# Retention followed by a multiplicative feed-forward layer: three w_out loads moved to ScalarE's queue, first weight products reordered

## Chip, core and metric

The kernel runs on one core of a Trainium2 chip. Its engines work side by side, each on its own list of instructions in program order: TensorE (PE in the profile: matmuls and transposes into PSUM; PEld is its weight load), VectorE (DVE), ScalarE (ACT), GpSimd (POOL) and SyncE (SP, which here only issues DMAs). The metric is the device time in microseconds (us). The time before is the median of three runs.

## What is computed

The first part is a recurrent retention over 4 batches, 8 heads, 768 tokens and head size 64, the second a feed-forward layer with a product of two projections, on 3072 tokens:

```python
gamma = 1.0 - 2.0 ** (-5.0 - np.arange(H))
for t in range(S):
    state = gamma * state + einsum('bhd,bhe->bhde', k[:, :, t], v[:, :, t])
    y[:, :, t] = scale * einsum('bhd,bhde->bhe', q[:, :, t], state)
x = y.transpose(0, 2, 1, 3).reshape(3072, 512)
a = x @ w1                # 512 x 1024
b = x @ w2                # 512 x 1024
h = (a * b) @ w3          # 1024 x 1024
out = h @ w_out           # 1024 x 512
```

All inputs and the output are float32; the matmuls take float16.

## The kernel before

**Tiling.** The tokens are cut into 12 chunks of 256, three to a batch. For each chunk the kernel computes retention as masked scores plus a carried state, then the products with w1 and w2, their elementwise product, and one last product. Since nothing stands between w3 and w_out, it multiplies these two once, at the start: W3O = w3 @ w_out, 1024 x 512, kept as eight tiles of 128 rows (`W3O[f]`).

**How W3O is made (lines 257 to 298).** Blocks of w3 and w_out come in as float32, 512 KB each, in staging tiles `st`: `r0` to `r7` are 128 rows of w3 (`load_rows`, line 107), `wo0` to `wo3` are 256 rows of w_out, two to a partition (`load_wo`, line 112). For each w3 block f there are these steps:

- `cast_w3(f, engs)` casts it to float16 (`w3h`, line 61 through `copy`; "vs" means the left half on VectorE and the right half on ScalarE).
- `turn_w3(f, bank)` turns it with eight transposes on TensorE (line 274).
- `turned_w3(f, eng)` copies the turned block from PSUM to SBUF (`w3t`, line 61).
- `w3_mm(f, i)` multiplies it with w_out block i, which `cast_wo(i, eng)` has cast (`wo`); two matmuls of 512 columns, line 290. Four of these, i = 0 to 3 in any order, sum up one `W3O[f]`, which `w3_out` copies out.

So `w3_mm(f, i)` needs both the turned block f and the cast block i. "S0", "X0", "K" and so on are names of PSUM banks.

**What sets the order.** The schedule is written out by hand (lines 696 to 1375): each engine executes its instructions in the order in which these calls emit them, and waits where its operand is not there yet. Lines 696 to 728 emit the loads: each of the `fetch` calls is one or more DMAs, all issued by SyncE, in this order: r4, wo0, r1, r2, wo1, r5, wo2, r3, r6, r7, k0, wo3, q0 (four DMAs), v0, r0, q1 (four), k1, v1, then the blocks of w1 and w2, then later tokens. There are 18 staging tiles. Lines 729 to 848 are the stage in which W3O is made, later mixed with the retention of chunks 0 and 1. `warm(m)` (line 674) issues m matmuls on zeros whose results nobody reads. `identity`, `numbers`, `arguments` and `tables` (lines 730 to 733) prepare constants; `tables` is the first thing on ScalarE: five activations of the function Exp (lines 233 and 235). `late_numbers` and `step_decays` are further constants on GpSimd.

Of the kernel before, what the change touches and what calls it, by code (L numbers as in the profile page):

```python
# [20 lines left out]
def kernel(  # L21
# [11 lines left out]
    nc = tc.nc  # L33
# [26 lines left out]
    def copy(eng, dst, src):  # L60
        {"v": nc.vector.tensor_copy, "g": nc.gpsimd.tensor_copy, "s": nc.scalar.copy}[eng](dst, src)  # L61

    def split(engs, dst, src):
        w = 1024 // len(engs)
        for j, eng in enumerate(engs):
            copy(eng, dst[:, j * w : (j + 1) * w], src[:, j * w : (j + 1) * w])
# [4 lines left out]
    def bank(tag, shape, dtype=FP):  # L71
        return psum.tile(shape, dtype, tag=tag, name="ps" + tag)
# [3 lines left out]
    def new_stage():  # L76
        return stage.tile([128, 1024], FP, tag="st", name="st")
# [4 lines left out]
    def load(nm, n, via=None):  # L82
        via = via or nc.sync
        b, c = divmod(n, PER)
        t = new_stage()
        src = source[nm][b, :, c * T : (c + 1) * T, :]
        if nm == "q" and n < EO:
            for a in range(NP):
                via.dma_start(
                    t[a : 128 : NP, :].rearrange("u (r x) -> u r x", r=2),  # L90
                    src[2 * a : 2 * a + 2, :, :].rearrange("r (u j) d -> u r (j d)", j=8),
                )
        elif nm == "q" or n < EO:
            via.dma_start(
                t[:, :].rearrange("p (h x) -> p h x", x=2 * D), src.rearrange("h (p t) d -> p h (t d)", t=2)
            )
        else:
            for s in range(2):
                via.dma_start(  # L99
                    t[:, s * 512 : (s + 1) * 512].rearrange("p (h d) -> p h d", d=D),  # L100
                    src[:, s * 128 : (s + 1) * 128, :].rearrange("h i d -> i h d"),
                )
        tok_in[nm, n] = t

    def load_rows(src, i):
        t = new_stage()
        nc.sync.dma_start(t[:, :], src[i * 128 : (i + 1) * 128, :])  # L107
        return t

    def load_wo(i):  # L110
        t = new_stage()
        nc.sync.dma_start(
            t[:, :].rearrange("p (t n) -> p t n", t=2),
            moe_w_out[i * 256 : (i + 1) * 256, :].rearrange("(p t) n -> p t n", t=2),
        )
        return t

    w3_st, wo_st, w_st = {}, {}, {}

    def fetch(names):  # L120
        for x in names.split():
            kind, i = x[:-1], int(x[-1])
            if kind == "r":
                w3_st[i] = load_rows(moe_w3, i)
            elif kind == "wo":
                wo_st[i] = load_wo(i)
            elif kind in ("w1", "w2"):
                w_st[kind, i] = load_rows({"w1": moe_w1, "w2": moe_w2}[kind], i)
            else:
                load(kind, i)  # L130
# [19 lines left out]
    def need(*x):  # L150
        assert done.issuperset(x)
# [26 lines left out]
    def late_numbers():  # L178
        done.add("late_numbers")

        nc.gpsimd.iota(tok_i[:, :, :], pattern=[[128, 2], [0, H]], base=1 - 128, channel_multiplier=1)
        for g in range(2):
            nc.gpsimd.iota(
                pos_i[:, g, :, :].rearrange("p s (t i) -> p s t i", t=2), pattern=[[128, 2], [1, 2], [2, 32]],
                base=1 - 128 + 64 * g, channel_multiplier=0,
            )
        nc.gpsimd.memset(keep64[:, :], 1.0)
        for g in range(2):
            rows = slice(g * 64, g * 64 + 64)
            nc.gpsimd.affine_select(  # L190
                out=keep64[rows, :], in_=keep64[rows, :], compare_op=GE, fill=0.0,
                base=0, pattern=[[1, 2], [2, 32]], channel_multiplier=-1,
            )
# [43 lines left out]
    def step_decays():  # L237
        done.add("decays")
        for h in range(H):
            r, p = (h % 2) * 64, h // 2  # L240
            nc.gpsimd.memset(GS[r : r + 64, p, :], gam[h] ** T)
# [18 lines left out]
    def cast_wo(i, eng):  # L260
        done.add(("wo", i))
        split(eng, WO[i][:, :, :].rearrange("p a n -> p (a n)"), wo_st[i][:, :])

    def cast_w3(f, eng):
        w3h[f] = att.tile([128, 1024], HP, tag="kq"[len(w3h_tags) % 2] + "16", name="w3h", bufs=3)
        w3h_tags.append(f)
        split(eng, w3h[f][:, :], w3_st[f][:, :])

    def turn_w3(f, tag):
        need("identity")  # L270
        src, ps = w3h.pop(f), bank(tag, [128, 1024], HP)
        for g in range(8):
            c0 = g // 2 * 256 + g % 2
            nc.tensor.transpose(ps[:, g * 128 : (g + 1) * 128], src[:, c0 : c0 + 255 : 2], ident16[:, :])  # L274
        w3p[f] = ps

    def turned_w3(f, eng):
        w3t[f] = fsb.tile([128, 1024], HP, tag="pa", name="w3t", bufs=8)
        copy(eng, w3t[f][:, :], w3p.pop(f)[:, :])

    def w3_mm(f, i, tag=None, first=False, last=False):
        need(("wo", i))
        if first:
            acc[f] = bank(tag, [128, DM])
            w3n[f] = 0
        w3n[f] += 2
        assert last == (w3n[f] == 8)
        for r in range(2):
            g = 2 * i + r
            nc.tensor.matmul(  # L290
                acc[f][:, :], lhsT=w3t[f][:, g * 128 : (g + 1) * 128], rhs=WO[i][:, r, :],
                start=(first and r == 0), stop=(last and r == 1),
            )
# [377 lines left out]
    def warm(m, tag="X1"):  # L671
        ps = bank(tag, [128, 512])
        for _ in range(m):
            nc.tensor.matmul(ps[:, :], lhsT=zeros[:, 0:128], rhs=zeros[:, :], start=True, stop=True)
# [15 lines left out]
    def evac(w, n, u, eng="s"):  # L690
        if w == "a":
            a_evac(n, u, ab.pop((w, n, u)), eng)
        else:
            b_evac(n, u, ab.pop((w, n, u)))

    fetch("r4")
    fetch("wo0")
    fetch("r1")
    fetch("r2")
    fetch("wo1")  # L700
    fetch("r5")
    fetch("wo2")
    fetch("r3")
    fetch("r6")
    fetch("r7")
# [32 lines left out]
    warm(3, "F2")  # L738
    turned_w3(4, "v")
    cast_wo(0, "s")  # L740
    warm(1, "F2")
    step_decays()
    cast_w3(1, "v")
    w3_mm(4, 0, "S0", first=True)
    cast_w3(2, "gs")
    turn_w3(1, "S1")
    warm(3, "F2")
    turned_w3(1, "v")
    turn_w3(2, "X0")
    warm(2, "F2")  # L750
    cast_wo(1, "g")
    w3_mm(1, 0, "S1", first=True)
    w3_mm(1, 1)
    warm(1, "F2")
    turned_w3(2, "v")
    w3_mm(2, 1, "X0", first=True)
    cast_wo(2, "g")
    cast_w3(5, "sv")
    late_numbers()
    w3_mm(4, 1)  # L760
    turn_w3(5, "X1")
    turned_w3(5, "v")
    w3_mm(1, 2)
    cast_w3(3, "s")
    w3_mm(2, 2)
    w3_mm(5, 2, "X1", first=True)
# [1 line left out]
    w3_mm(5, 0)  # L768
    turn_w3(3, "K")
    fetch("v3")  # L770
    w3_mm(4, 2)
    w3_mm(2, 0)
    turned_w3(3, "s")
    turn_w3(6, "F0")
    w3_mm(5, 1)
# [630 lines left out]
```

## Time and profile before

| | |
|---|---|
| median of 3 runs | 181.64 us (180.94 to 182.09) |
| the profiled execution's own time | 181.46 us |
| its span in the profile | 179.7 us |
| TensorE busy in the span | 172.8 us (96%) |
| VectorE, ScalarE, GpSimd busy | 100.1, 67.9, 64.5 us |
| moved by DMA | 40.22 MB, mean 224 GB/s |
| first DMA issue, SyncE | 0.81 us after the start |

The span is the time between the first and last instruction that the profile records; 1.76 us of the execution lie outside it. A line of the timeline gives the start, the duration, the engine, the line of the kernel, the operation, what it writes and reads, and in brackets how long the engine was idle before and what ended this idle time. The chain of waits starts from the last instruction and goes back, at each step to what released it.

### The profile page before, as it was taken

To read this page: it belongs to the slowest core of one execution; us is meant where nothing else is said; L and a number is where in the kernel's file an instruction comes from. 1 tells how busy PE (TensorE), PEld (TensorE's weight loads), DVE (VectorE), ACT (ScalarE), POOL (GpSimd) and SP (SyncE) were. 2 spreads that over 40 slices of the span, in tenths; PEclk is the share of its full clock that TensorE was granted. 3 is DMA by queue.
4 is the path that set the end of the run, shared out by engine and by line. 5 is a ranking of instruction groups with operands and counts; after the bars stand their busy time and mean duration, and the time that the engine had idled before them with its cause. 6 is when DMAs were issued, how large, how long until landed. Compare 5 with 4: busy or idle time off the path is not lost.

```text
span 179.7 us, 6033 instructions
## 1 busy us (share of the span) xinstructions
PE 172.8 (96%) x2626; PEld 123.7 (69%) x2626; DVE 100.1 (56%) x172; ACT 67.9 (38%) x120; POOL 64.5 (36%) x93
## 2 busy tenths in 40 slices
PE   7699999999999999999999999999999999999993
PEld 2245556578856785885877858768688587786872
DVE  2342779762966487548367384464654836634330
ACT  4425537790237332322314314232232231332422
POOL 7545056576242752724437045062450500000000
PEclk9999999999999999999999999999999999999999
DMA  5999999999999999999999999999999982250303
GB/s 201 364 420 364 357 312 364 406 348 233 177 259 239 213 173 221 202 196 237 150 209 266 196 237 231 210 280 209 237 255 264 108 277 67 81 156 4 117 0 117
DMA packets 80025, 40.22 MB, mean 224 GB/s; under 512 B 59392, under 2 KB 73984, under 8 KB 80000
## 3 DMA queue, kind: packets, MB, share of 16 engines
q1 hardware_dynamic: 80000, 39.85, 92.2%
q8 instruction: 20, 0.33, 0.8%
q14 instruction: 5, 0.04, 0.1%
HBM read 29.36 MB, written 6.29 MB: 198 GB/s over the span
## 4 chain that ended last, share of the span: by engine, by line
PE 75%; DMA 12%; SPq 4%; ACT 3%; POOL 2%; DVE 1%; issue 1%; POOLq 0%
PE psF L573 38%; PE psF L630 20%; DMA st<-in_moe_w_out_dram 5%; DMA st<-in_v_dram 4%; DMA st<-in_k_dram 3%; SPq L99 2%; PE psX L509 2%; PE psK L290 2%; PE psF L290 2%; PE psX L290 2%; PE psX L536 2%; PE psS L394 1%; ACT pa L61 1%; POOL v L69 1%; PE psS L290 1%; SPq L107 1%
## 5 line engine op out<-in xcount | busy, mean ns | idle before, releaser
L573 PE MATMUL psF<-xt,w 128*128 128x256 f16 x640 | 71.8, 273 | 0.0
L573 PEld LDWEIGHTS <-w 128*128 128x128 f16 x640 | 62.5, 98 | 9.4
L69 DVE TENSOR_TENSOR ht<-pa,psF 128x512 f16<-128x512 f32 x43 | 29.6, 687 | 43.1 <-PE psF L573 42.0
L61 ACT COPY pa<-psF 128x512 f32<-128x512 f32 x43 | 25.1, 586 | 44.1 <-PE psF L573 38.4
L630 PE MATMUL psF<-w3o,ht 128*128 128x512 f16 (+2 forms) x184 | 38.4, 361 | 0.0
L69 POOL TENSOR_TENSOR v<-st,VN 128x1024 f16<-128x1024 f32 x10 | 19.0, 1904 | 40.0 <-DMA st<-in_v_dram 39.9
L630 PEld LDWEIGHTS <-ht 128*128 128x128 f16 x208 | 19.1, 98 | 18.8
L648 ACT ACTIVATE osb<-psF 128x512 f32<-128x512 f32 (+2 forms) x22 | 12.3, 559 | 35.4 <-PE psF L630 35.4
L554 DVE TENSOR_TENSOR xt<-psX,YN 128x512 f16<-128x512 f32 x19 | 12.8, 723 | 5.7 <-PE psX L536 5.7
L609 PEld LDWEIGHTS <-w 128*128 128x128 f16 x128 | 11.9, 98 | 2.9 <-ACT w L61 0.6
L414 DVE TENSOR_TENSOR am<-psS,keep 128x512 f16<-128x512 f32 x19 | 12.2, 681 | 0.7 <-PE psF L394 0.7
L61 POOL CAST q<-st 128x1024 f16<-128x1024 f32 x9 | 9.4, 1042 | 7.4 <-DMA st<-in_q_dram 4.4
L61 POOL CAST k<-st 128x1024 f16<-128x1024 f32 x9 | 9.6, 1064 | 6.7 <-DMA st<-in_k_dram 3.7
L290 PEld LDWEIGHTS <-w3t 128*128 128x128 f16 x64 | 5.8, 97 | 7.0 <-issue 1.2
L609 PE MATMUL psF<-xt,w 128*128 128x256 f16 x56 | 9.5, 272 | 0.0
L69 POOL TENSOR_TENSOR t<-s,GS 128x256 f16<-128x256 f32 x8 | 5.8, 729 | 6.6 <-DVE s L69 6.6
L61 POOL CAST w<-st 64x1024 f16<-64x1024 f32 (+2 forms) x6 | 6.5, 1084 | 3.1 <-DMA st<-in_moe_w_dram 2.9
L509 PE MATMUL psX<-qT,t 64*64 64x64 f16 (+1 forms) x296 | 7.5, 199 | 0.0
L274 PEld LDWEIGHTS <-w3h 128*128 128x128 f16 x64 | 4.0, 98 | 4.5 <-DVE w3h L61 3.0
L69 POOL TENSOR_TENSOR v<-st,VS 128x1024 f16<-128x1024 f32 x2 | 3.9, 1933 | 8.7 <-DMA st<-in_v_dram 8.7
L61 ACT CAST w3h<-st 128x512 f16<-128x512 f32 (+1 forms) x5 | 3.5, 704 | 9.1 <-DMA st<-in_moe_w_dram 9.1
L509 PEld LDWEIGHTS <-t 64*64 64x64 f16 x320 | 4.9, 106 | 2.9 <-issue 2.5
(125 smaller groups left out, 192.1 us busy)
## 6 DMA issues: line engine op xcount, KB each, us to landing
st<-in_moe_w_dram SPq DMA_DIRECT2D x16, 512.0 KB, 9.0
st<-in_k_dram SPq DMA_DIRECT2D x20, 256.0 KB, 6.0
st<-in_q_dram SPq DMA_DIRECT2D x10, 512.0 KB, 6.6
st<-in_v_dram SPq DMA_DIRECT2D x20, 256.0 KB, 4.7
out_dram<-osb SPq DMA_DIRECT2D x9, 512.0 KB, 5.7
st<-in_moe_w_out_dram SPq DMA_DIRECT2D x4, 512.0 KB, 10.1
st<-in_k_dram SPq DMA_DIRECT2D x2, 512.0 KB, 5.7
st<-in_q_dram SPq DMA_DIRECT2D x8, 128.0 KB, 6.0
```

Source lines behind the costliest of these rows:

```text
L61: {"v": nc.vector.tensor_copy, "g": nc.gpsimd.tensor_copy, "s": nc.scalar.copy}[eng](dst, src)
L69: (nc.vector if eng == "v" else nc.gpsimd).tensor_tensor(dst, a, b, op)
L99: via.dma_start(t[:, s * 512 : (s + 1) * 512].rearrange("p (h d) -> p h d", d=D), src[:, s * 128 : (s + 1) * 128, :].rearrange("h i d -> i ...
L274: nc.tensor.transpose(ps[:, g * 128 : (g + 1) * 128], src[:, c0 : c0 + 255 : 2], ident16[:, :])
L290: nc.tensor.matmul(acc[f][:, :], lhsT=w3t[f][:, g * 128 : (g + 1) * 128], rhs=WO[i][:, r, :], start=(first and r == 0), stop=(last and r = ...
L414: nc.vector.tensor_tensor(t[:, :, :, :].rearrange("p a s i -> p (a s) i"), ps[:, :, :, :].rearrange("p a s i -> p (a s) i"), keep64[:, :]. ...
L509: nc.tensor.matmul(dst, lhsT=TS[n, c][half(r), a, :], rhs=rhs, start=((g, o) not in begun), stop=False, skip_group_check=True,)
L554: nc.vector.tensor_tensor(XT[n][:, :, :].rearrange("p a (s x) -> p (a s) x", s=2)[:, :, g * 64 : (g + 1) * 64].rearrange("p k (i t) -> p k ...
L573: nc.tensor.matmul(ps[:, i, :], lhsT=W[d][:, f * 128 : (f + 1) * 128], rhs=XT[n][:, d, :], start=(i == 0 and d == 0), stop=(i == 1 and d = ...
L609: nc.tensor.matmul(rows_ps[w, n, uh][j // 2][:, j % 2, :], lhsT=W[d][:, f * 128 : (f + 1) * 128], rhs=XT[n][:, d, :], start=(first and j % ...
L630: nc.tensor.matmul(ps[:, :], lhsT=HT[n][:, f, tb * 128 : (tb + 1) * 128], rhs=W3O[f][:, c0:c1], start=(f == 0), stop=(f == 7),)
L648: nc.scalar.activation(o_tile(n, tb)[:, c0:c1], o_ps.pop((n, tb, c0, c1))[:, :], AF.Copy, scale=final_scale)
```

## The change

`load_wo` and `fetch` get an argument for the engine that issues the DMA. The loads of wo0, wo1 and wo2 are issued by ScalarE; their calls stand where they stood, ahead of `tables`, so they are the first three DMAs in ScalarE's program. SyncE issues r4, r1, r2, r5, r3, r6, r7, k0, wo3 and all the rest. The order of the first casts, transposes and products is changed; none is added or left out, and the number of zero matmuls stays at 18.

```diff
-    def load_wo(i):
+    def load_wo(i, via):
         t = new_stage()
-        nc.sync.dma_start(
+        via.dma_start(
...
-    def fetch(names):
+    def fetch(names, via=nc.sync):
...
-                wo_st[i] = load_wo(i)
+                wo_st[i] = load_wo(i, via)
...
     fetch("r4")
-    fetch("wo0")
+    fetch("wo0", nc.scalar)
     fetch("r1")
     fetch("r2")
-    fetch("wo1")
+    fetch("wo1", nc.scalar)
     fetch("r5")
-    fetch("wo2")
+    fetch("wo2", nc.scalar)
     fetch("r3")
     fetch("r6")
     fetch("r7")
...
     warm(3, "F2")
     turned_w3(4, "v")
     cast_wo(0, "s")
-    warm(1, "F2")
     step_decays()
     cast_w3(1, "v")
+    warm(1, "F2")
     w3_mm(4, 0, "S0", first=True)
-    cast_w3(2, "gs")
+    warm(3, "F2")
+    cast_wo(1, "g")
     turn_w3(1, "S1")
-    warm(3, "F2")
+    warm(1, "F2")
     turned_w3(1, "v")
-    turn_w3(2, "X0")
-    warm(2, "F2")
-    cast_wo(1, "g")
+    w3_mm(4, 1)
     w3_mm(1, 0, "S1", first=True)
     w3_mm(1, 1)
-    warm(1, "F2")
+    cast_w3(2, "vs")
+    cast_wo(2, "g")
+    warm(2, "F2")
+    w3_mm(4, 2)
+    turn_w3(2, "X0")
     turned_w3(2, "v")
+    w3_mm(1, 2)
+    late_numbers()
+    cast_w3(5, "sv")
     w3_mm(2, 1, "X0", first=True)
-    cast_wo(2, "g")
-    cast_w3(5, "sv")
-    late_numbers()
-    w3_mm(4, 1)
     turn_w3(5, "X1")
+    w3_mm(2, 0)
     turned_w3(5, "v")
-    w3_mm(1, 2)
     cast_w3(3, "s")
     w3_mm(2, 2)
     w3_mm(5, 2, "X1", first=True)
...
     w3_mm(5, 0)
     turn_w3(3, "K")
     fetch("v3")
-    w3_mm(4, 2)
-    w3_mm(2, 0)
     turned_w3(3, "s")
     turn_w3(6, "F0")
     w3_mm(5, 1)
```

## The prediction

> **What bounds the kernel now.** I read the page first, to see which engine fills the span.
>
> ```profile
> span 179.7 us, 6033 instructions
> ...
> PE 172.8 (96%) x2626; PEld 123.7 (69%) x2626; DVE 100.1 (56%) x172; ACT 67.9 (38%) x120; POOL 64.5 (36%) x93
> ...
> PE   7699999999999999999999999999999999999993
> ...
> DMA  5999999999999999999999999999999982250303
> ```
>
> TensorE is full from the third slice (4.5 us each) to the end, and so are the DMA engines for three quarters of the span. Only the first slices hold idle TensorE time, and there DMA is full too. The change lies there. Second, the chain of waits, in order of time, to see where the dense part begins and what it hangs on before.
>
> ```profile
> 3.72 9.41 DMA st<-in_moe_w_out_dram
> 13.13 0.05 issue
> 13.19 1.05 POOL wo L61
> 14.23 0.04 issue
> 14.28 0.59 PE psS L290 x2
> ...
> 59.67 1.91 POOL v L69
> 61.59 0.04 issue
> 61.63 0.19 PE psX L442
> ```
>
> The chain starts with wo2: landed at 13.13 us, cast on GpSimd until 14.23, and from 14.28 TensorE leads. At 61.63 TensorE once more waits for data (a cast of v, 0.16 us in the timeline). After that it is contiguous to the end. So a delay of TensorE's list at 20 us comes out at the end almost in full, less that 0.16. Third, the timeline of the first 21 us, for what the reordered calls wait for.
>
> ```profile
> 0.81 1.28 ACT L233 ACT_TABLE_LOAD   x1 [0.81 <-PEq L1390]
> 3.60 0.21 ACT L233 ACTIVATE VS<-vs_x 128x16 f32<-128x16 f32 x1 [1.51 <-DVE vs_x L69]
> 8.03 0.69 DVE L61 CAST w3h<-st 128x1024 f16<-128x1024 f32 x1 [1.73 <-DMA st<-in_moe_w_dram]
> 13.19 1.04 POOL L61 CAST wo<-st 128x1024 f16<-128x1024 f32 x1 [1.53 <-DMA st<-in_moe_w_out_dram]
> 16.00 0.61 PE L274 MATMUL psK<-ident,w3h 128*128 128x128 f16 x8
> 16.65 1.01 ACT L61 COPY w3t<-psK 128x1024 f16<-128x1024 f16 x1 [1.17 <-PE psK L274]
> 17.31 0.61 PE L274 MATMUL psF<-ident,w3h 128*128 128x128 f16 x8
> 20.10 0.62 ACT L61 CAST wo<-st 128x512 f16<-128x512 f32 x1 [1.93 <-DMA st<-in_moe_w_out_dram]
> ```
>
> Casts that wait for a load start when it lands. Read so, the landings are r4 4.19, wo0 by 5.60 (its cast follows the last table activation without a wait), r1 8.03, r2 9.31, wo1 10.62, r5 11.87, wo2 13.19, r3 14.44, r6 15.72, wo3 20.10: some 1.27 us for each 512 KB, the pace of full DMA engines (400 to 426 GB/s from 6 to 15 us in the windows of one us). I call these times slots. The wo3 cast ends at 20.72 and its first product starts at 20.81, so TensorE could be at most 0.09 us earlier there unless wo3 itself lands earlier. From 14.28 to 20.81 it has no gap: 0.43 us from one `w3_mm` to the next, 0.45 for one `turn_w3`.
>
> **The change, part by part.**
>
> *Issue on SyncE.* Three issues of 0.41, 0.49 and 0.45 us leave its queue; the later ones move up by as much. SyncE was 7.5 us ahead of the casts there (wo2 issued at 3.72, landed at 13.13), so this is worth 0: the full DMA engines cover it. If they were not full, 1.35 us could be had.
>
> *Issue on ScalarE.* Three DMAs ahead of its table load. By SyncE's rows, 0.81 + 0.41 + 0.49 + 0.45 and gaps of 0.05 end at 2.3; with 1.28 for the table load 3.58. VS waited for VectorE until 3.60: 0. Behind it stand YS (1.71 us) and the cast of wo0, which must be done by 7.7 (below). The other bound is the longest such issue, 4.16 us at 9.30: then the cast of wo0 ends near 10.3, `w3_mm(4, 0)` starts 2.6 us later, and, since the 18 zero matmuls take up some of it, `w3_mm(4, 2)` about 0.75 later. I take 0, since the nearest rows are those of the same blocks at the same time.
>
> *Order of the landings.* No row of before shows two data queues: queue q1 has all 80000 data packets. Bytes and engines stay the same, so I take it that the slots stay and only their owners change. Shared evenly from the start, r4 and wo0 have the slot 5.60, r1 and wo1 9.31, r2 and wo2 11.87, r5 13.19, then r3 as before. Served one by one in order of issue it would be r4 4.19, wo0 5.60, r1 8.03, wo1 9.31, r2 10.62, wo2 11.87: wo2 is the same in both.
>
> The bounds on the slots: the DMA rows of 2 to 6 us move 315, 352, 340 and 283 GB/s against 401 after, 0.31 MB less, or 0.78 us at that rate. If two queues closed this gap, all slots would come 0.78 earlier. The other end is a ScalarE queue that starts after the table load (a rival below): wo2 one slot later, 1.32.
>
> *The new order on TensorE.* r4 5.60, cast 0.69 on VectorE, turn, copy 0.69 from 7.03 to 7.72; with wo0 cast by 6.64, `w3_mm(4, 0)` at 7.78. r1 9.31, cast to 10.0, turn at 10.06, copied by 11.41; wo1 cast on GpSimd to 10.35; `(4,1)` 10.72, `(1,0)` 11.47, `(1,1)` to 12.33. wo2 11.87, cast 1.04, so `(4,2)` at 12.97, where before the corresponding start was 14.28.
>
> From there to `w3_mm(3, 2)`, which started at 18.19 before: eight products and four turns (2, 5, 3, 6), 8 x 0.43 + 4 x 0.45 = 5.24, so 18.21 without waits. Before it was seven products and two turns, 3.91, from 14.28. The earlier wo2 thus buys nothing: turns 2 and 5, which were done before 14.28, now stand behind it. The waits come on top:
>
> - `(2,1)` needs turn 2 copied: turn 13.40, its last result 0.62 later at 14.02 (as in the row at 16.00), VectorE 14.06 to 14.75, start 14.81; only `(1,2)` covers it, until 14.28: 0.53.
> - `(5,2)` needs turn 5 copied: turn 15.24, copy 15.90 to 16.59, start 16.65 against 16.55: 0.10.
> - `(3,2)` needs turn 3 copied on ScalarE. Before, the copy ran from 16.65 to 17.66 under `(4,2)`, `(2,0)`, turn 6 and `(5,1)`. Two of the four are gone. Turn 3 at 17.51, copy 18.17 to 19.18, start 19.24 against 18.84: 0.40.
>
> Each of these waits is 0 at best and, if VectorE is late with a cast queued ahead of the copy (0.43, its half of r5 or r2), 0.43 longer at worst. I take the worked values, from the rows of the same operations. Behind the copy of turn 3 on ScalarE its half of r7 and of wo3 are queued; the latter lands at 20.10, so nothing more.
>
> *GpSimd and VectorE.* GpSimd gives up its half of the cast of r2 (0.61 us), VectorE takes it over (0.43). `late_numbers` (some 1.2 us on GpSimd) now follows the cast of wo2 directly, as it did before, and ends near 14.1, ahead of the half of r6 at 15.72. GpSimd is then idle until v0 at 24.27, which covers all of this: 0. Without that cover the 1.2 us would delay r6, and turn 6 with it.
>
> Sum: 0.02 + 0.53 + 0.10 + 0.40 = 1.05 us later at `(3,2)`. After that nothing is reordered; the list is contiguous and DMA has all later blocks in the same slots. Less the 0.16 at 61.63: +0.89. The profiled execution is 181.46 us (span 179.7, 1.76 around it), 0.18 under the median; so 182.35 for it, and 182.5 against the median.
>
> **Rivals.**
>
> *ScalarE's queue is served ahead.* If wo2 has slot 10.62, with r2 still at 11.87, r2 decides: its ScalarE half is cast by 12.49, turn 2 at 12.55, copied by 13.90, `(2,1)` 13.96, turn 5 14.39, `(5,2)` 15.80, turn 3 16.66, copy to 18.33, `(3,2)` 18.39: 0.20 later than before, less 0.16: +0.04, 181.7 on the median, not slower. For it: only three blocks in that queue. Against: nothing in the rows shows a preference. It decides once wo2 lands before 11.4. The Trainium skill (DMA: Bandwidth & Descriptors, section on queues, rings and completion order) says that each DMA engine takes turns between its queues packet by packet; by that the pairs share their slots and this rival falls. No row of before can show it.
>
> *The stream starts faster.* Two queues close the gap of the first 6 us; all slots come 0.78 earlier and so does everything above: 182.5 - 0.78 = 181.7. For it: 315 and 283 GB/s at the start. Against: the DMA busy shares of these us are 0.88 to 1.00 already. With the rival above as well, 180.9.
>
> *The table load goes first.* At 0.81 it was ScalarE's first instruction. If it stays first, the three DMAs go out from 2.1; wo0 shares slot 8.03 with r1, wo1 10.62 with r2, wo2 13.19 with r5. `(4,2)` starts at 14.29, 1.32 later than above, with the same waits behind it: +2.21, 183.8 on the median, slower by over 1%. It decides as soon as wo2 lands after 12.9. The Trainium skill (ScalarE: Activation LUTs, the step-by-step section on the stages) says that the load is placed right before the activation that needs it; by that the DMAs go first and the sum above holds. The row at 0.81 agrees with both, as no DMA stood there.
>
> *The loads are as before and the order costs nothing.* It would need all three copies hidden; only one product or one turn stands ahead of each, so this is in the rest.
>
> **How the numbers follow.** The likeliest is the sum, 182.5, with a range of its own from 182.0 to 183.0 (one of the waits gone, or 0.43 longer): 0.50. Served ahead, 181.7: 0.18. Faster stream, 181.7: 0.12. Table load first, 183.8: 0.15. The rest 0.05: both gains together, or the long issue on ScalarE. From 181.0 to 183.9 these leave out about 1 in 10. About 1%, 1.8 us, is what a measurement of this kernel can tell from no change: faster than 179.8 takes more than the two gains together, 0.03; slower than 183.46 is the table load first or the long issue, 0.17; the remaining 0.80 lie within.
>
> **What would show it.** Right: SyncE issues W3's blocks in a row from 0.81; the cast of wo2 starts near 11.9 on GpSimd; TensorE waits before the first products of blocks 2 and 3, 0.5 and 0.4 us; `w3_mm(3, 2)` starts near 19.2 and the last stretch from 61.6 is 0.9 later. Wrong: wo3 landing well before 20.1, wo2 before 11.4 or after 12.9, ScalarE's VS after 3.7, no wait at the copy of turn 3, or a TensorE wait at 61.6 that is longer than 0.16, which would mean that later loads moved too.

## The result, and the profile after

The changed kernel takes 183.8 us (median of 21 runs, 182.23 to 186.88) against 181.76 us (21 runs, 180.94 to 183.03): ratio 1.0089, interval 1.0066 to 1.0112, some 1.6 us slower (1.2 to 2.0 by the interval), 0.9%. The ratio leaves out four runs of the changed kernel that took over 1.5% more than its fastest, which is why the medians lie further apart, 2.0 us. The time lies at the upper end of the predicted range of 181.0 to 183.9, above the predicted 182.5 and outside the 182.0 to 183.0 that the sum had for itself. Its profiled execution took 185.37 us, more than the median; so a second trace of each kernel was taken (`after_again`, 183.71 us, `before_again`, 182.54 us), and of each cause it is said which traces show it.

The page of the changed kernel, the lines that answer to those shown of before:

```profile
span 183.6 us, 6035 instructions
...
PE 175.0 (95%) x2626; PEld 124.4 (68%) x2626; DVE 100.8 (55%) x173; ACT 67.6 (37%) x120; POOL 63.6 (35%) x92
...
PE   7799999999999999999999999799999999999991
...
q1 hardware_dynamic: 79568, 38.28, 92.1%
q10 hardware_dynamic: 432, 1.57, 2.1%
q8 instruction: 20, 0.33, 0.7%
q14 instruction: 6, 0.05, 0.1%
```

ScalarE's three blocks (1.57 MB) now have a queue of their own, q10. TensorE's row has one new weak slice, at 115 to 119 us, far behind the change. Then the start of the changed kernel, from its timeline:

```profile
0.81 1.38 ACTq L112 DMA_DIRECT2D st<-in_moe_w_out_dram  x3
2.21 1.28 ACT L233 ACT_TABLE_LOAD   x1 [2.21 <-issue]
3.58 0.22 ACT L233 ACTIVATE VS<-vs_x 128x16 f32<-128x16 f32 x1
5.30 0.70 DVE L61 CAST w3h<-st 128x1024 f16<-128x1024 f32 x1 [1.52 <-DMA st<-in_moe_w_dram]
6.88 2.13 PE L674 MATMUL psF<-zeros 128*128 128x512 f16 x4
7.83 0.70 DVE L61 CAST w3h<-st 128x1024 f16<-128x1024 f32 x1
10.60 0.61 PE L274 MATMUL psS<-ident,w3h 128*128 128x128 f16 x8
10.83 1.04 POOL L61 CAST wo<-st 128x1024 f16<-128x1024 f32 x1 [1.41 <-DMA st<-in_moe_w_out_dram]
13.30 0.59 PE L290 MATMUL psS<-wo,w3t 128*128 128x512 f16 x2
...
14.18 0.59 PE L290 MATMUL psS<-wo,w3t 128*128 128x512 f16 x2
...
15.13 0.61 PE L290 MATMUL psX<-wo,w3t 128*128 128x512 f16 x2 [0.35 <-DVE w3t L61]
18.49 1.01 ACT L61 COPY w3t<-psK 128x1024 f16<-128x1024 f16 x1 [4.32 <-PE psK L274]
...
18.73 0.60 PE L290 MATMUL psX<-wo,w3t 128*128 128x512 f16 x2
...
19.55 1.04 PE L290 MATMUL psK<-wo,w3t 128*128 128x512 f16 x4 [0.23 <-ACT w3t L61]
```

The three issues, the table load and VS stand where they were worked out (the table load from 2.21 to 3.49, VS at 3.58). wo2 is cast from 10.83, 2.36 earlier than before, and yet `w3_mm(4, 2)`, the row at 13.30, is no earlier than its forecast of 12.97; `w3_mm(3, 2)`, the row at 19.55, is 1.36 later than before. Here r1 was cast by 8.53, but its turn starts at 10.60: the zero matmuls ahead of it ran at 0.43 us each until 10.24 and at half of that afterwards (in `after_again` from 4.42 on: the four that take 2.13 here take 1.24 there).

Last, where the chain of waits of the changed kernel shows something that the one of before does not:

```profile
22.55 2.04 DVE q L61
...
117.76 1.08 issue
```

The cast of q0 took 0.69 before. At 117.76 TensorE stands still for 1.08 us and waits for nothing that the profile shows.

One more difference is behind the last matmul, which starts at 176.39 us of 179.67 before and at 179.60 of 183.64 after: 3.28 against 4.04 us to the end of the span. I call this **the end stretch**. SyncE's wait for the last store is the whole of the difference: it ends 2.29 us after the start of the last matmul before, 3.06 after. The DMA view from 1.4 us after the last matmul, in 40 slices of 0.055 us; before:

```profile
GB/s 117 135 307 293 335 349 224 154 14 0 0 0 0 0 0 0 0 0 0 0 0 0 0 0 0 0 0 0 0 0 0 0 0 0 0 0 0 0 0 0
...
q1 hardware_dynamic: 159, 0.11, 15.2%
```

and after:

```profile
GB/s 140 131 196 293 349 293 429 126 56 0 0 0 0 0 0 14 14 28 28 14 14 0 0 0 0 0 0 0 0 0 0 0 0 0 0 0 0 0 0 0
...
q1 hardware_dynamic: 162, 0.11, 15.1%
q14 instruction: 1, 0.01, 1.5%
```

Before, the store is out in nine slices. After, a remainder follows six slices later: eight of its 128 packets of 768 bytes, an even share for one of 16 DMA engines, end between 2.31 and 2.55 us after the last matmul, the others by 1.92. In between lies one 8 KB packet of the instruction queue q14, from 1.74 to 2.28; the first of the eight starts when it ends.

### The profile page after: what moved, and what is told of

Same layout as the page of the kernel before. It is cut to its first block, busy times and chain, and to the rows that moved or that the text cites. A ratio compares the mean times of both kernels' runs of the same rounds, so it can differ in the third digit from the quotient of the medians.

```text
span 183.6 us, 6035 instructions
## 1 busy us (share of the span) xinstructions
PE 175.0 (95%) x2626; PEld 124.4 (68%) x2626; DVE 100.8 (55%) x173; ACT 67.6 (37%) x120; POOL 63.6 (35%) x92
## 3 DMA queue, kind: packets, MB, share of 16 engines
q10 hardware_dynamic: 432, 1.57, 2.1%
## 4 chain that ended last, share of the span: by engine, by line
PE 89%; DVE 3%; DMA 2%; ACT 1%; issue 1%; DVEq 0%
PE psF L573 38%; PE psF L630 20%; PE psF L609 3%; DMA st<-in_moe_w_dram 2%; PE psX L509 2%; PE psX L609 2%; PE psX L630 2%; PE psK L290 2%; PE psF L674 2%; PE psX L536 2%; PE psS L394 2%; PE psF L290 2%; PE psS L290 1%; PE psS L609 1%; PE psX L290 1%
## 5 line engine op out<-in xcount | busy, mean ns | idle before, releaser
L536 PE MATMUL psX<-am,v 64*64 64x64 f16 (+1 forms) x336 | 6.1, 197 | 1.1 <-issue 1.1
L69 DVE TENSOR_TENSOR t<-psK,t 128x256 f16<-128x256 f32 x15 | 6.3, 418 | 0.4
```

The source lines that it names most:

```text
L69: (nc.vector if eng == "v" else nc.gpsimd).tensor_tensor(dst, a, b, op)
L536: nc.tensor.matmul(o, lhsT=v16[n][half(g), t, h * D : (h + 1) * D], rhs=rhs, start=((g, c) not in begun), stop=(n >= EO or t == 1), skip_g ...
```

## The experiments

Twelve kernels were run. The ratio is to runs of before made together with the kernel, with its 95% interval; the medians of those runs were 181.76 to 182.27, so the ratio is not the quotient of two rows. In the rows with `_again`, which are one execution each, it is left out. The next three columns are of each kernel's trace: the start of `w3_mm(3, 2)`, the start of the last matmul, and the end stretch; then the time at which q14's last 8 KB packet starts, from the last matmul. The last column is the ratio in us, less what the end stretch is longer than 3.28: what is left for the list itself (for the change with the mean of its two traces). It is as uncertain as the ratio, some 0.4 to 0.8 us either way and 1.2 for order_only, which has four runs, and it takes the end stretch of one trace for that of all runs. Of the three traces with before's order and one queue, the first is the earliest at the last matmul (176.39, 177.45, 177.42).

| kernel | median us (runs) | ratio | (3,2) | last matmul | end stretch | q14 | rest |
|---|---|---|---|---|---|---|---|
| before | 181.76 (21) | 1 | 18.19 | 176.39 | 3.28 | 4.25 | 0 |
| before_again | 182.54 (1) | | 18.42 | 177.45 | 3.28 | 4.25 | |
| after | 183.8 (21) | 1.0089 [1.0066, 1.0112] | 19.55 | 179.60 | 4.04 | 1.74 | 0.8 |
| after_again | 183.71 (1) | | 18.84 | 177.79 | 4.18 | 1.70 | |
| queue_only | 183.1 (10) | 1.0049 [1.0018, 1.0079] | 18.59 | 177.88 | 4.17 | 1.72 | 0.0 |
| order_only | 184.96 (4) | 1.0163 [1.0094, 1.0231] | 19.82 | 179.12 | 3.28 | 4.52 | 3.0 |
| after_warm11 | 183.54 (10) | 1.0069 [1.003, 1.0109] | 18.26 | 177.12 | 4.04 | 1.67 | 0.5 |
| table_first | 182.99 (10) | 1.0045 [1.0013, 1.0078] | 19.18 | 177.44 | 3.33 | -2.97 | 0.8 |
| warm11_swap | 182.5 (10) | 1.0022 [0.9993, 1.0052] | 18.55 | 176.41 | 4.15 | 1.75 | -0.5 |
| fit_order | 182.23 (12) | 1.0017 [0.9988, 1.0046] | 17.01 | 175.77 | 4.05 | 1.70 | -0.5 |
| fit_order_sync | 183.31 (10) | 1.0034 [0.999, 1.0078] | 18.91 | 179.33 | 3.28 | 4.25 | 0.6 |
| warm11_cover | 182.67 (8) | 1.0055 [1.0021, 1.0088] | 18.74 | 176.92 | 4.09 | 1.71 | 0.2 |
| fit_swap | 182.2 (12) | 1.0018 [0.9982, 1.0055] | 17.87 | 175.86 | 4.19 | 1.74 | -0.6 |
| before_swap | 181.62 (12) | 0.9999 [0.9966, 1.0032] | 18.14 | 177.42 | 3.29 | 4.28 | 0.0 |

The end stretch was found last, when all kernels had been run; the expectations below do not know of it.

**First theory and rival.** The start of the change showed TensorE at half rate for 5 us longer than before. Theory of the clock: r4 lands 1.1 us later because it shares its slot with wo0, TensorE idles, and it reaches its full rate late. Rival, the theory of the prediction: the new order costs what was summed, whatever the clock.

*queue_only.* The loads as in the change, the order of before:

```diff
-    fetch("wo0")
+    fetch("wo0", nc.scalar)
...
-    fetch("wo1")
+    fetch("wo1", nc.scalar)
...
-    fetch("wo2")
+    fetch("wo2", nc.scalar)
```

> The old order of calls; only the issue of wo0, wo1 and wo2 moves to ScalarE. Clock theory (sharing with wo0 makes r4 land near 5.3 us, TensorE idles after its eight zero matmuls and its matmuls then stay at 0.43 us for 512 columns until some 10 us): 183.0 to 183.6 us, about 1.5 over before. Order theory (the time is lost in the waits for the copies of turned blocks in the new order): 181.4 to 182.0 us, as before.

183.1: the clock theory's time, but not by its way. r4 landed at 5.34, as late as in the change, and the full rate was there at 4.37. So r4's late landing does not by itself delay the full rate. The loss of 0.9 us (0.3 to 1.4) is as much as the end stretch of its trace is longer, 0.88.

*order_only.* The change with all loads on SyncE:

```diff
-    fetch("wo0", nc.scalar)
+    fetch("wo0")
...
-    fetch("wo1", nc.scalar)
+    fetch("wo1")
...
-    fetch("wo2", nc.scalar)
+    fetch("wo2")
```

> The new order of calls; SyncE issues all loads in the old sequence. Clock theory: r4 lands near 4.2 us, no long idle time, 512 columns take 0.22 us from about 5 us on; what is left are the waits for the copies, at most 0.9: 181.8 to 182.6 us. Order theory: nearly the whole loss stays, 182.7 to 183.6 us.

184.96, on the side of the order theory and 1.4 us beyond its range, from four runs alone. In its timeline the sum of the prediction can be read off:

```profile
13.56 0.59 PE L290 MATMUL psS<-wo,w3t 128*128 128x512 f16 x2 [0.59 <-POOL wo L61]
15.38 0.60 PE L290 MATMUL psX<-wo,w3t 128*128 128x512 f16 x2 [0.36 <-DVE w3t L61]
19.82 1.04 PE L290 MATMUL psK<-wo,w3t 128*128 128x512 f16 x4 [0.23 <-ACT w3t L61]
```

From `w3_mm(4, 2)` to `w3_mm(3, 2)` it is 6.26 us, with a wait at the copy of turn 2 and one at the copy of turn 3. In the change it is 6.25, in `after_again` 6.25, with eleven zero matmuls 6.25; the prediction had 12.97 to 19.24, 6.27. Before it was 14.28 to 18.19, 3.91, so the order's price is 2.35 us, and an earlier `w3_mm(4, 2)` pays some of it back: here 0.72, since wo2 landed at 12.41, which leaves 1.63 at `w3_mm(3, 2)`. The rest of the 3.0 in the table is not accounted for in full; a stop of 0.8 us near 118, of which more below, is part of it in this trace, and the two slowest of the four runs have a granted clock of 0.99 where the others have 1.0, as in fit_order_sync below. With two queues the order costs 0.7 us (1.0089 against queue_only's 1.0049; the intervals overlap).

*after_warm11.* The change, with three zero matmuls more at the start, which bridge the idle time:

```diff
-    warm(8)
+    warm(11)
```

> The changed kernel with eleven instead of eight zero matmuls at the start, which fill TensorE until r4 is cast (6.05 us). Clock theory: 512 columns take 0.22 us by 7 us at the latest, the first products come 1 to 2 us earlier, 181.6 to 182.5 us. Order theory: 183.3 to 184.0 us, as the changed kernel.

183.54, the order theory's time: filling the idle time does not make the kernel faster. The full rate came at 5.95, `w3_mm(4, 2)` at 12.01 and `w3_mm(3, 2)` at 18.26, as late as before's and 1.29 ahead of the change; the median hardly moved. The gain was given back at 34 us, as its timeline shows:

```profile
33.61 1.03 POOL L61 CAST w<-st 64x1024 f16<-64x1024 f32 x1 [1.38 <-DMA st<-in_moe_w_dram]
...
33.76 1.43 DVE L61 CAST w<-st 64x1024 f16<-64x1024 f32 x1
...
35.34 0.38 PE L609 MATMUL psK<-xt,w 128*128 128x256 f16 x2 [0.89 <-ACT w L61]
```

and the timeline of before at the same place:

```profile
33.68 0.69 DVE L61 CAST w<-st 64x1024 f16<-64x1024 f32 x1
...
34.26 1.04 POOL L61 CAST w<-st 64x1024 f16<-64x1024 f32 x1 [1.37 <-DMA st<-in_moe_w_dram]
34.52 0.38 PE L609 MATMUL psK<-xt,w 128*128 128x256 f16 x2
```

VectorE casts half of block 1 of w1, for which TensorE waits, GpSimd half of block 3, which starts when its load lands. With GpSimd's load there 0.65 earlier, GpSimd starts first, and VectorE's 0.69 becomes 1.43: it ends at 35.19, 0.55 after GpSimd's end at 34.64. The product starts 0.15 after that, as it does before (34.37 and 34.52); the bracket names ScalarE, whose second cast happens to end at 35.27.

*table_first.* The change, with the table load put ahead of ScalarE's DMAs by a one-column activation:

```diff
+    first_exp = const.tile([128, 1], FP, name="first_exp")
+    nc.scalar.activation(first_exp[:, :], zeros[:, 0:1], AF.Exp)
...
     fetch("r4")
```

> The changed kernel with one small activation of Exp ahead of ScalarE's three DMAs, so that the table load and this activation (some 1.6 us) stand before them and r4 has the DMA engines to itself at first. Clock theory: r4 near 4.2 us, full rate of TensorE from about 5 us; wo2 near 13 us is then late: 182.4 to 183.8 us. Order theory: the slots move back by one, 184.5 to 185.5 us.

182.99, in the clock theory's range, and faster than the change, where the rival of the prediction said slower. r4 landed alone again (4.28), wo2 at 11.79 instead of 13, since only wo0 came late (6.70). The rival also took the issues to wait for the table load; here it runs from 0.81 to 2.09, and they stand at 1.25, 1.68 and 2.16. The 0.8 us by which it beats the change is the end stretch: it is also the only kernel with two queues without a longer end stretch. Its DMA view at the same place, 1.4 us after its last matmul:

```profile
GB/s 140 131 251 307 335 363 266 140 42 0 0 0 0 0 0 0 0 0 0 0 0 0 0 0 0 0 0 0 0 0 0 0 0 0 0 0 0 0 0 0
...
q1 hardware_dynamic: 162, 0.11, 15.5%
```

Here q14's packet had gone 2.97 us before the last matmul. So a second queue does not make the end late by itself. The traces hold 191 records of ScalarE in the kernels with one queue (packet after the end), 194 with its three DMAs (packet under the last store), 195 here (packet before it). Between this kernel and fit_order below, ScalarE's records are the only ones whose number differs (195 and 194), and the packet starts at -2.97 in one and 1.70 in the other. So it is read as the packet that brings ScalarE's last instructions; no view names its engine.

*before_again and after_again.* Both kernels once more, for the trace; no edit.

> The kernel before once more, for a second trace. If its slow landings (r1 at 8.01 instead of some 6.9 us) belong to its single queue, r1 lands near 8 and wo3 near 20 us again; if they were a chance of one execution, wo3 lands near 19 us. If the moment at which TensorE reaches full rate is a chance, it need not be 4.9 us again. No stall of TensorE near 116 us if that stall belongs to the changed kernel's timing. Time as before, 181 to 183 us.

> The changed kernel once more. If the late full rate of TensorE (10.24 us) follows from r4 landing late, it is near 10 us again and w3_mm(3, 2) near 19.5 us; if it is a chance, full rate comes between 4 and 7 us and w3_mm(3, 2) near 18.3 us. A stall of TensorE near 116 us again if it belongs to this kernel's timing. 182.5 to 184.5 us.

The full rate came at 7.09 in `before_again` and at 4.42 in `after_again`, so its moment varies from execution to execution; 6.25 and the end stretch stayed. wo3 landed late again with one queue (20.31 in `before_again`). The cast of w1 collided in `before_again` too (1.56 instead of 0.69, product at 35.62). In `after_again` another pair met, the cast of r1 with that of wo1, which now land together:

```profile
8.23 1.04 POOL L61 CAST wo<-st 128x1024 f16<-128x1024 f32 x1 [1.03 <-DMA st<-in_moe_w_out_dram]
8.46 1.36 DVE L61 CAST w3h<-st 128x1024 f16<-128x1024 f32 x1 [0.85 <-DMA st<-in_moe_w_dram]
```

Again VectorE's end, 9.82, is 0.55 after GpSimd's, 9.27.

**Second theory: colliding casts.** *warm11_swap* is after_warm11 with the two casts of w1 swapped:

```diff
-    cast_w(W1, "w1", 1, "vs")
+    cast_w(W1, "w1", 1, "gs")
...
-    cast_w(W1, "w1", 3, "gs")
+    cast_w(W1, "w1", 3, "vs")
```

> The changed kernel with eleven zero matmuls at the start and the halves of two w1 blocks exchanged: GpSimd casts the half of w11, VectorE that of w13, so that GpSimd is idle while VectorE casts. If the two casts slow each other when they overlap (1.43 instead of 0.69 us in the trace with eleven zero matmuls), the product that waited until 35.34 us starts near 34.6 and the time falls by 0.5 to 0.7 us, to some 182.9; if that wait has another cause, nothing changes: 183.5 us.

182.5, and the wait of 0.89 is gone: the product starts at 34.76. The ratio is 0.0047 lower than that of after_warm11 (0.85 us), but the intervals overlap.

*fit_order.* Two queues and a new order for the loads as they now land: turn 2 ahead of `w3_mm(4, 2)`, and two products or more behind each turn before its copy is needed. Three zero matmuls have moved to the start, which now has eleven, and a few casts have moved with the matmuls (not shown):

```diff
-    w3_mm(4, 2)
     turn_w3(2, "X0")
     turned_w3(2, "v")
+    w3_mm(4, 2)
...
-    w3_mm(2, 1, "X0", first=True)
     turn_w3(5, "X1")
-    w3_mm(2, 0)
+    w3_mm(2, 0, "X0", first=True)
+    w3_mm(2, 1)
...
-    w3_mm(2, 2)
-    w3_mm(5, 2, "X1", first=True)
-    w3_mm(5, 0)
     turn_w3(3, "K")
+    w3_mm(2, 2)
     turned_w3(3, "s")
+    w3_mm(5, 0, "X1", first=True)
+    w3_mm(5, 2)
```

> Both queues, eleven zero matmuls at the start, and another order of the first products: turn 2 ahead of the products with wo2, and each copy of a turned block covered by at least two products. Order theory (the waits for the copies of blocks 2, 5 and 3 and the turns behind wo2 are the loss): w3_mm(3, 2) near 17.2 us, 1 us earlier than before, and 180.8 to 181.8 us. Queue theory (two queues cost time by themselves, through w_out taking bandwidth from w3): 182.5 to 183.5 us.

`w3_mm(3, 2)` at 17.01, 1.18 ahead of before. `w3_mm(4, 2)` waits 0.49 for the cast of wo2, until 12.16, and from there on nothing waits: the waits for the copies can be avoided. But the time is that of before. In this trace most was given back at once, to a load that no one had moved. From its timeline:

```profile
21.36 0.59 PE L290 MATMUL psF<-wo,w3t 128*128 128x512 f16 x2
21.92 0.69 DVE L61 CAST q<-st 128x1024 f16<-128x1024 f32 x1 [1.84 <-DMA st<-in_q_dram]
22.67 0.51 PE L358 MATMUL psX<-perm,q 128*128 128x128 f16 x6 [0.71 <-DVE q L61]
```

q0 lands at 21.80, no earlier than before, where its cast started at 21.64, and TensorE waits 0.71. In the other traces with two queues whose landing of q0 can be read it lands between 20.17 and 20.53. The packets tell why: all but three of its 256 packets of 2 KB end by 19.77, and the last three at 20.82, 21.04 and 21.25, behind a 16 KB packet of the instruction queue q8 that runs from 19.48 to 20.61. It is the picture of the last store once more. In fit_swap below, which has this order, q0 was not held up and the median is the same, so this wait is not what keeps fit_order from being faster. Its last matmul is still 0.62 ahead of before's, and the end stretch takes 0.76.

*fit_order_sync.* fit_order with all loads on SyncE (the three edits shown at order_only).

> The order of calls of fit_order and its eleven zero matmuls, but all loads issued by SyncE in the old sequence. If the second queue brings the loads forward (wo3 at 18.8 to 19.1 us with it in all traces so far, at 19.4 to 20.3 without), wo2 lands at 12.4 to 13.4 instead of 11.0 us, w3_mm(3, 2) starts near 18.4 to 19.4 instead of 17.0 us, and the time is 183 to 184 us. If the second queue is worth nothing and the fitted order did it alone: 182.0 to 182.5 us, as fit_order.

183.31, as expected if the queue matters, but the interval holds 1, and in this trace TensorE fell back to half rate from 11.71 to 15.12 and stood still for 1.84 us at 139.62. It shows `w3_mm(3, 2)` 1.9 later than fit_order and cannot say how much of that is the queue's: inconclusive. The fall in rate is no chance of this one execution: its granted clock is 0.99, and eight of the ten runs have 0.988 to 0.991, against 0.995 and more with fit_order. Two of order_only's four have it too. What brings it about was not tried.

*warm11_cover.* after_warm11 with two products put back behind turn 3, where they stood before:

```diff
-    w3_mm(4, 2)
     turn_w3(2, "X0")
...
     turn_w3(5, "X1")
-    w3_mm(2, 0)
...
     fetch("v3")
+    w3_mm(4, 2)
+    w3_mm(2, 0)
     turned_w3(3, "s")
```

> The changed kernel with eleven zero matmuls at the start and two products, (4, 2) and (2, 0), put back behind turn 3. If the missing cover of the copies is what the order costs, turn 2 starts near 11.5 us, the wait of 0.23 us at (3, 2) is gone, w3_mm(3, 2) starts near 17.6 instead of 18.3 us, and the time falls by 0.4 to 0.9 us against the kernel with eleven zero matmuls (183.5), less where the casts of the w1 halves meet. If the cover does not matter: 183.5 us and w3_mm(3, 2) at 18.3 us.

A miss: `w3_mm(3, 2)` at 18.74, not 17.6. The wait at turn 3 went, but now the copy of turn 5 was waited for as well as that of turn 2 (0.35 each in its timeline), and r1's cast met GpSimd (1.25). The ratio is 0.0014 lower than that of after_warm11: no difference.

*fit_swap and before_swap.* The same swap of the casts of w1 in fit_order and in the kernel before (edit as in warm11_swap).

> fit_order with one more edit: GpSimd casts its half of block 1 of w1, VectorE its half of block 3 (the two swapped). Theory of the casts (a cast on VectorE that starts under an operation of GpSimd ends 0.55 us after that operation, so a load that lands earlier can make it later): no gap of TensorE before the first product with block 1 of w1, which starts at 34.1 to 34.5; w3_mm(3, 2) at 17.0 to 17.6 as in fit_order; 181.2 to 181.9 us, ratio to before 0.996 to 1.001. Rival (the casts of one block of w1 are not worth anything in the median): 182.2 as fit_order, ratio 1.0017.

> The kernel before with the same swap of the two casts of w1 and nothing else. Theory of the casts: the collision is there without the change too, in some executions (1.56 instead of 0.69 us in the second trace of before, none in the first), so the swap takes 0 to 1.1 us off an execution: 181.2 to 181.7 against 181.8 of before, ratio 0.995 to 0.999; the first product with block 1 of w1 at 34.3 to 34.8 without a gap ahead of it. Rival (the collision belongs to the change, and two of the traces show it by chance): ratio 0.999 to 1.002.

182.2 and 181.62: no difference in either. The casts no longer meet (products at 34.07 and 34.36), but in the kernel before this is worth nothing that 12 runs can tell, and in fit_swap the casts of r1 and wo1 met instead (1.51). The rival has it for these two kernels: the collision is a way in which a single execution is late. What part it has in the change's 1.6 us is not shown, since warm11_swap's gain lies within the noise.

## Why the prediction was right, and where it was not

**Right in direction, in range and in its main step, low by a term.** The forecast of +0.89 us is below the interval of 1.2 to 2.0. That 183.8 is still in the range is owed to the room made for the rival of the table load, whose price was 183.8 and which did not occur; this is luck. *The new order on TensorE* is the step that carried the forecast, and it holds: 6.27 us worked out, 6.25 or 6.26 in all six traces of this order. Its waits hold one by one. From start to start, as the sum counts, the product at 14.18 is over at 14.61 and the next starts at 15.13: 0.52 for 0.53; the one at 18.73 is over at 19.16, the next starts at 19.55: 0.39 for 0.40. (The brackets say 0.35 and 0.23, since they count from the end of the last matmul in the array.) fit_order's trace avoids these waits. What the change loses without the end stretch, 0.8 us in the median and in table_first, is near the +0.89 of the sum. That agreement is partly luck: it rests on `w3_mm(4, 2)` at 12.97, and the traces of this order with two queues have 12.01 to 13.30 for it. The sum had it wait for the cast of wo2, until 12.91; in the trace of the change that cast was done at 11.87, and TensorE came late to it, behind its half-rate zero matmuls.

*Issue on ScalarE*: right to 0.02 us (VS at 3.58 for 3.60), if the price is looked for at the start. But "I take 0", as the price of this issue for the whole kernel, is **the step that failed**. With three instructions more in ScalarE's list, q14's last packet starts under the last store and not behind the end of the kernel, and this costs 0.75 to 0.9 us: in both traces of the change, in all eight traces with 194 records, in none of the six with 191 or 195. queue_only's loss is of this size. The trace of before shows the packet at 4.25 us after the last matmul; nothing in the prediction asked what sets its place. That the packet holds up one DMA engine's part of the store is read from the order of the packets: in each of the eight traces the last eight packets of the store come behind it, the first within 0.01 us of its end. A kernel that adds idle instructions to ScalarE and changes nothing else was not tried. Nor was fit_order with such an instruction, which by the table could be some 0.5 us ahead of before, an estimate within the noise.

*Order of the landings*: the sharing is as chosen. Pairs land together: r4 5.27 and wo0 5.45, r1 7.81 and wo1 8.16, r2 10.38 and wo2 10.78. The Trainium skill (DMA: Bandwidth & Descriptors, the section on queues, rings and completion order), by which a DMA engine takes turns between its queues, agrees with this, and the rival of the preferred queue falls. "The slots stay" failed, and two signs that the prediction had named as wrong came in, wo2 before 11.4 (10.78) and wo3 well before 20.1: wo3 landed at 18.79 instead of 20.08, and between 18.78 and 19.12 in every trace with two queues, against 18.96 to 20.31 in those with one. So the rival of the faster stream occurred, and bought nothing: TensorE's own list, its clock and VectorE decided in its place, and the loads that came earlier met other casts. Why one queue is slower in some executions stays open, but the traces show where: a load's landing is recorded as 16 updates of a semaphore, and from r1 on these lie 1.3 to 1.8 us apart in the traces of before, `before_again` and before_swap, 0.8 in order_only, 0.4 to 0.5 in fit_order_sync and under 1.0 with two queues. wo3's first update came at 18.71 in before and at 18.38 in the change. So a part of each load falls behind, more than the whole stream does.

*The table load goes first*: it did not (2.21), and forced to, it was no loss: the rival's +2.21 took the late slot of wo0 for all three blocks. *The 0.16 at 61.63* vanished, but not for the reason given, a list that comes later. The offset of TensorE's list to before's falls by some 0.2 us there in all 13 other traces, also in fit_order and fit_swap, which come 0.4 us earlier. The wait belonged to that one trace of before. Behind it the list of the change is 1.34 later, 0.46 in `after_again`: as forecast, what is lost by 20 us comes out behind 61.6 almost in full.

**Not in the sum.** The moment of TensorE's full rate (in the first trace of the change about 0.7 us of its 1.36 at `w3_mm(3, 2)`, from the comparison with `after_again`) and the stop near 117 us. The latter, 0.7 to 1.3 us from the start of one matmul to the next (the chain's 1.08 counts from the end of the one before), is in both traces of the change, in queue_only, order_only and fit_order_sync, and in none of before's. It is at the same matmul in all five. There TensorE goes on 1.4 to 1.6 us after a 16 KB packet of the other instruction queue, q8, has ended; this packet starts 1.6 to 2.0 us before the stop, and in the nine others 2.8 to 3.6 us before that matmul. What makes it late was not tried, and how many of the executions without a trace have the stop is not known. The 0.8 that is left of the change's loss may hold some of it; table_first has 0.8 left too, and no stop in its trace.

## What to carry to other kernels

An edit's price may lie where nothing was edited: count the instructions that it adds to a queue, and look in the trace for the packets of the instruction queues near the last store and near stalls that the chain calls "issue". An earlier load is worth what the engine behind it has free, and it moves the casts that start on its landing; look for what they now run beside. Before explaining a difference between two traces, take a second trace of each: here TensorE's full rate and the meeting of the casts of w1 came and went between traces of one and the same kernel.

## What the runs showed of the hardware

A cast on VectorE from SBUF to SBUF that starts under an operation of GpSimd ends a fixed time after it: 0.55 us for 1024 columns (35.19 after 34.64, 9.82 after 9.27, and q0's of the changed kernel 24.57 after 24.02; where its own 0.69 ends later than that, it takes its 0.69), 0.28 for 512 (12.03 after 11.75 in `after_again`), instead of running 0.69 or 0.42. Its copy from PSUM beside such an operation kept its 0.69 (11.24 in the changed kernel). The Trainium skill (SBUF — State Buffer, on the port pair that VectorE and GpSimd share) calls it an exclusive lock, held for the whole instruction; these rows agree.

Instruction packets are not always free. The Trainium skill (Runtime: NRT & Kernel Launch, the section on instruction fetch mechanics) calls the cost of crossing a block of instructions mostly hidden; here an 8 KB packet under the last store goes with 0.75 to 0.9 us, in eight traces of eight, and a late 16 KB one with 0.7 to 1.3 us of TensorE. In fit_order a 16 KB packet under the load of q0 goes with a landing 1.3 to 1.6 us later than in the other traces with two queues.

The moment at which a 512-column matmul goes from 0.43 to 0.22 us varied from 3.99 to 10.24 us over 14 traces, with eight or eleven zero matmuls at the start of all of them. The granted clock does not show this step: in the changed kernel it is 1.00 in every us from 5 to 10, while these matmuls take 0.43. It does show the later fall in fit_order_sync, with 0.50 in every us from 12 to 15.
